# A build-time order made anew: another length for an exponential, another table of turns, three shifts at the end

## The chip, the cores and the metric

The kernel runs on one core of one Trainium2 chip. The metric is the device time of one execution in microseconds (us), as the median of several runs. The engines are called TensorE (PE in the profile, with its weight loads as PEld), VectorE (DVE), ScalarE (ACT), GpSimd (POOL) and SyncE (SP).

## The reference

The output mixes an attention block and a gated feed-forward block by a gate for each row. S = 2048 rows, D = 512 columns, 32 heads of 16, F = 1792. All inputs are bf16.

```python
x = A_x
g = sigmoid((x * gate_w).sum(-1, keepdims=True))
qkv = (x @ wqkv).reshape(B, S, 3, H, Dh).transpose(2, 0, 3, 1, 4)
q, k, v = qkv[0], qkv[1], qkv[2]
p = softmax(einsum("bhqd,bhkd->bhqk", q, k) * Dh ** -0.5)
a = einsum("bhqk,bhkd->bhqd", p, v).transpose(0, 2, 1, 3).reshape(B, S, D) @ wo
b = (silu(x @ w_gate) * (x @ w_up)) @ w_down
return g * a + (1 - g) * b
```

## The kernel before

**The work.** The attention is cut into units: 4 blocks of 512 queries by 8 groups of four heads, 32 units in all. Each unit runs over 16 key tiles of 128 keys, so there are 512 key tiles. For each, the scores (keys on the partitions, 4 x 512 columns) go through an exponential, and the result is multiplied with the values. The values carry a column of ones, so that the denominators come with the sums. Projections (kp, qp, vp), the feed-forward block (gu, dps) and the output projection (ops) are side work of TensorE, cut into pieces.

**Two ways to an exponential.** A key tile of ScalarE takes two score pairs: two score matmuls side by side fill the 1024 columns of an s_t tile (there are two such tiles in PSUM), and one ACTIVATE turns it into an e_t tile. Then a round of four value matmuls adds it to o_ps. A key tile of VectorE takes four d_t tiles of 512 columns. VectorE evicts each with a multiply and an add to 16-bit integers, whose bits are an approximate exponential in bf16. That result then becomes either four copies (three passes that add one of SHIFTS, and four rounds of value matmuls) or two copies (two passes that mask bits and one product, and two rounds). GpSimd takes strips of some passes and of the products. A d_t tile may ride in the same TensorE round as an s_t pair. The copies lie in c_t, kaug or wd_t, whichever buffer is free.

**The order.** Each engine's instructions are put in one fixed order when the program is built. A planner (the object plan) keeps a clock for each engine and books a cost on it with every instruction that it places: 0.217 us for a round on TensorE and FLIP = 0.107 for a change between score rounds and column rounds, 0.6 for an eviction on VectorE, and ACT_US for the exponential of an s_t tile on ScalarE. These clocks decide what is placed next. The pair emitter waits for the time at which the planner believes the s_t bank free (s_end), and before that fills TensorE's room with value rounds, side pieces and d_t tiles. The function v_unit decides whether another key tile goes to VectorE: it does so if VectorE's clock with its work in hand and a lead lies before the end of ScalarE's remaining tiles of the unit, reckoned from plan.act with TILE_US = 1.9 a tile. The chip sees none of these costs. It sees the order and the split between the engines.

```python
        def exp():
            act(out=e_t[:], in_=s_t[:], func=ACT.Exp, scale=inv_sqrt_dh)
            plan.act = max(plan.act, ready) + ACT_US
            s_end[i] = plan.act + SLOT
...
                end = plan.act + (left - 1) * TILE_US + ((hi[au] - at_) * TILE_US if vu > au else 0.0)
                busy = sum(v.cost for v in vops) + 0.6 * (len(owed) + len(d_wait))
                if plan.dve + busy + (LEAD if vu < UNITS - 1 else LAST) + {"h": -2.0, "i": 2.0}.get(turn_of(pairs[0]), 0.0) <= end:
                    return vu
```

**The table of turns.** TURNS holds two characters for each score pair, in the order in which the pairs are placed: one read by turn_of, one by way_of. A dot leaves the planner's rule as it is. A letter bends one rule at that pair. Of turn_of: a, b, c change how far TensorE may overrun the free bank; d lets no d_t tile ride along; e lets one take a bank that would be kept for side work; f and g change the credit for side work; h and i shift the lead in v_unit; j, k and o change which value round goes first; s holds back side pieces. Of way_of: f and g bear on two copies or four; l, m, o, d, r and u change what VectorE does first; n, q and t what GpSimd takes; v and w how much work VectorE may have in hand; x and y how early and how many d_t tiles may be placed.

**The end.** The last unit's last two key tiles are cut by halves of the queries. What follows them is placed by a small list of steps, each with an engine, a cost and the steps that it comes after with a gap: rc1 and rc0 are reciprocals of denominators, sp1 and sp0 their spread over the partitions by TensorE, n their product with the sums, p the last products with the output weights, c the copies out. LAST_HALF names the steps of the second half of the queries, which are preferred. Rounds of a rest of the output projection (al_o) are put between the steps where they fit.

Of the kernel before, what the change touches and what calls it, by code (L numbers as in the profile page):

```python
# [54 lines left out]
class Pacer:  # L55
# [30 lines left out]


TURNS = (
    ".......u................g.a.k...............i...a................n.....x...v..s................."
    "j............x.x....e....g.......r.r.g....c.c...a......x..................e....r.w.....y........"  # L90
    "......hn.x..............j.h.........if.....v.......m........k.............i....q..........a....."
    "....h.o..........r.........f..f.h.........gt.....uhm............................................"
    "....................j................................qb..g.r.............x.................y...."
    "........k.d............g.f......f..o...............w................hf................k..t...r.."
    "..........s.........h........w...f........................s............................g........"
    ".......g.......v...y...r........k......o........c..............................................."
    ".....d..........i.a......lo..g......e..t..e..v.......r.........................................."
    "............a..m....f...i.k......rk........x.......lk.............k..........d...............g.."
    "..............b....y........o......w.....u..e..f.....g....a....f.r..d.b.bl..............i.k....d"
    "...u....iq........k....ge................f..c....m..s...gu...mh..xbvj..x.wo...c.b..w.qbq.x..bw.."  # L100
    "bm.q..e.......cy...........r..o.....o.....h...........a..................u...w.w.......r..g....."
    "........b........gk..t...........f.xsykl...n..j.o...b...o....l.la......n......h...h..ddr..k.s.c."
    "a..g...rj.h...h....ds.....j...h......v...y.....l.....l....c..l...yb.i...ov.nb...i...a..l......k."
    ".u....k...elj.g...i.k.....j.o....lb.....fg.........qa.....c.a.fy..ku.r"
)


# [1 line left out]
def kernel(  # L109
# [86 lines left out]
    def act(*args, **kw):  # L196
        ordered(nc.scalar.activation(*args, **kw))  # L197
# [127 lines left out]
    plan = Plan()  # L325
# [5 lines left out]
    def spend(mode, mms, ready=0.0):  # L331

        plan.seq += 1
        work_at.append((plan.pe, mms))
        plan.pe = max(plan.pe + (FLIP if mode != plan.mode else 0.0), ready) + (0.226 if mode == "F" else 0.217) * mms
        plan.mode = mode
# [437 lines left out]
    def emit_pair(bs, ride=0):  # L774
# [17 lines left out]
# [4 lines that stand above are left out]
# [8 lines left out]
    KF = 2  # L804
# [6 lines left out]
    def emit_fin():  # L811
# [14 lines left out]
# [4 lines that stand above are left out]
# [36 lines left out]
        return TURNS[2 * n + 1] if 2 * n + 1 < len(TURNS) else "."  # L866

    exps = []
    ACT_US = 0.9167

    def flush_act(before=None):

# [408 lines left out]
    def spread_rows(p, rt, tqs=range(TQ), c0=0):  # L1281
        for tq in tqs:
            for j in range(4):
                mm(p[32 * j:32 * j + 32, c0 + tq * P:c0 + (tq + 1) * P],
                   lhsT=rt[:, 4 * tq + j:4 * tq + j + 1].broadcast_to([P, 32]), rhs=ident[:, :],
                   start=True, stop=True, tile_position=(0, 32 * j), skip_group_check=True)
# [4 lines left out]
    def last_rows(t):  # L1291
        cs = slice(t * P, (t + 1) * P)
        return lambda i: ((onc[QB - 1][:, i, cs], wo_t[:, i, :]) if i < NB - 1 else
                          (osbs[UNITS - 2][:, cs], wo_l[:, 0, :]) if i == NB - 1 else (ident[:, :], bblk[:, t, :]))
# [7 lines left out]
    rest = [(3, i) for i in range(NB + 1)]  # L1302

    def apart(p, w, r, start, stop):
        for j in range(4):
            mm(p[32 * j:32 * j + 32, 0:D], lhsT=w[:, 32 * j:32 * j + 32], rhs=r, start=start, stop=stop,
               tile_position=(0, 32 * j), skip_group_check=True)
# [504 lines left out]
    while au < UNITS:  # L1812
# [10 lines left out]
        if room > 0.02:  # L1823
# [29 lines left out]
            if room > 0.4 and not fin and closed in o_of and 0 < pvs[closed] and pv_left(closed) > 1 and (closed or pvs[0] != FT) and sum(  # L1853
                    w for t, w in work_at[-24:] if t > plan.pe - 3.0) < 6.5:

                for j in range(4):
                    mm(o_of[closed][32 * j:32 * j + 16, :], lhsT=vaug[:, 0, G * 4 * VC:], rhs=xT[:, 0, 0:QBW],
                       start=False, stop=False, tile_position=(0, 32 * j), skip_group_check=True)
# [58 lines left out]
    def fin_inv(h):  # L1917
        rt = work.tile([P, 4 * TQ], BF16, tag="rt", name="rt")
        recip16(rt[:, 8 * h:8 * h + 8], fin_l["p", h][:, 8 * h:8 * h + 8])
        fin_l["r", h] = rt  # L1920

    def fin_spread(h):
        spread_rows(fin_l["p", h], fin_l["r", h], (2 * h, 2 * h + 1), P - 2 * P * h)

    def fin_norm(tq, n=1):
        cs, c0 = slice(tq * P, (tq + n) * P), P + tq % 2 * P
        vec.tensor_tensor(out=on_l[:, cs], in0=osb[:, cs], in1=fin_l["p", tq // 2][:, c0:c0 + n * P], op=ALU.mult)
# [24 lines left out]
    LAST_HALF = ("os1", "dt1", "rc1", "sp1", ("n", 2), ("n", 3), ("p", 2), ("p", 3), ("v", 2 * KF - 1))  # L1952

    def step(name, engine, cost, f, *after):
        steps[name] = (engine, cost, f, after)
# [3 lines left out]
    step("os1", "A", 0.47, lambda: fin_copy(1), (("v", 2 * KF - 1), 0.25))  # L1959
    step("dt1", "F", 0.5, lambda: fin_dens(1), ("os1", 0.06))  # L1960
    step("rc1", "V", 0.22, lambda: fin_inv(1), ("dt1", 0.25))
    step("sp1", "C", 1.5, lambda: fin_spread(1), ("rc1", 0.3))
    for tq in (2, 3):
        step(("n", tq), "V", 0.23, lambda tq=tq: fin_norm(tq), ("sp1", 0.22))
        step(("p", tq), "C", 1.0, lambda tq=tq: fin_product(tq), (("n", tq), 0.06), (("l", tq), 0.0))
    step("dt0", "F", 0.5, lambda: fin_dens(0), ("os0", 0.06), ("s", 0.0))
    step("rc0", "V", 0.22, lambda: fin_inv(0), ("dt0", 0.25))
    step("sp0", "C", 1.5, lambda: fin_spread(0), ("rc0", 0.3))
    step("n0", "V", 0.37, lambda: fin_norm(0, 2), ("sp0", 0.22))
    for tq in (0, 1):  # L1970
        step(("p", tq), "C", 1.0, lambda tq=tq: fin_product(tq), ("n0", 0.06))
# [7 lines left out]
    al_at = lambda tq: s_end[1 - older] if "dt0" in over else 1e9  # L1979
    over["l", 2] = 0.0  # L1980
    now = {"V": plan.dve, "A": plan.act}
    while steps:
        able = {}
        for name, (engine, cost, f, after) in steps.items():
            if all(a in over for a, t in after):
                able[name] = max([now.get(engine, plan.pe)] + [over[a] + t for a, t in after])
        best = None
        for name, start in able.items():
            engine, cost = steps[name][:2]
            cost *= 0.217 if engine in "CF" else 1.0  # L1990
            if name not in LAST_HALF and any(able[o] + 0.06 < start + cost for o in able if o in LAST_HALF and (
                    steps[o][0] == engine or steps[o][0] + engine in ("CF", "FC"))):
                continue
            if best is None or start < best[0] - 0.02:
                best = start, name
        lim = min([max(plan.pe, max(over[a] + t for a, t in st[3])) for st in steps.values() if st[0] in "CF" and all(a in over for a, t in st[3])], default=1e9)
        if rest and not (best and best[0] <= plan.pe) and (best is None or best[1] != ("v", 2 * KF - 1)) and max(plan.pe, al_at(rest[0][0])) + 0.12 <= min(lim, 1e8):
            tq, i = rest.pop(0)
            if i == 0:
                a_ps.append(ps_s.tile([P, 2 * QBW], F32, tag="s", name="al_o"))  # L2000
            w, r = last_rows(tq)(i)
            apart(a_ps[tq], w, r, i == 0, False)
            spend("C", 1, al_at(tq))
            if not rest or rest[0][0] != tq:
                over["l", tq] = plan.pe
            continue
        start, name = best
        engine, cost, f, after = steps.pop(name)
        if engine in "CF":
            if name[0] == "v":  # L2010
                plan.pe = max(plan.pe, start)
                f()
                over[name[1]] = plan.pe
            else:
                f()
                spend(engine, cost, start)
            over[name] = plan.pe
        else:
            plan.dve = start
            f()  # L2020
            now[engine] = over[name] = start + cost
            plan.dve = now["V"]
# [34 lines left out]
```

## Time and profile before

| | |
|---|---|
| median of 3 runs | 742.37 us (741.66 to 742.51) |
| the profiled execution's own time | 742.09 us |
| its span, first to last instruction | 740.4 us |
| busy share of PE, DVE, ACT, POOL | 97%, 97%, 98%, 40% |
| exponentials on ScalarE (e_t from s_t) | 754, mean length 1098 ns |
| granted TensorE clock | 0.999 |

A row of the groups in the profile gives the source line, the engine, the operation, output and input by the program's names, their shapes and the count. Behind the first bar stand the busy time in us and the mean length of one in ns, behind the second the idle time of the engine just before these instructions, and what ended it. Nearly all instructions go through one helper for each engine, so the line numbers are those of the helpers (L194 TensorE, L197 ScalarE, L206 the others); groups are told apart by tile. An instruction's recorded length overlaps with the next one on the same engine, so lengths don't add up to time.

### The profile page before, as it was taken

The numbers are of one execution on the slowest core, as the hardware profiler recorded it, in microseconds if no ns is written. First come the engines' busy times: TensorE is split into PE (matmuls) and PEld (weight loads), VectorE is DVE, ScalarE is ACT, GpSimd is POOL, SyncE is SP. The second block draws the span as 40 slices with busy tenths as digits, with TensorE's granted clock in tenths as the row PEclk, the third lists the DMA queues.
The fourth block names the chain that finished last, engine by engine and source line by source line (L and its number), as shares of the span: only waits on it lengthen the run. The fifth ranks groups of instructions, "written<-read, shape, count | busy, mean of one in ns | idle before, by whom it ended". The sixth has DMA issues, their size and how long they took to land.

```text
span 740.4 us, 23142 instructions
## 1 busy us (share of the span) xinstructions
PE 721.8 (97%) x9296; PEld 213.6 (29%) x9296; DVE 715.5 (97%) x1223; ACT 728.4 (98%) x828; POOL 299.6 (40%) x370
## 2 busy tenths in 40 slices
PE   8999999999999999999999999999999999999997
PEld 3323222232222222322222222222222222222223
DVE  5999999999999999999999999999999999999995
ACT  7999999999999999999999999999999999999996
POOL 4044242234453336345444225544445255343441
PEclk9999999999999999999999999999999999999999
DMA  9001233355210012320200041302001231200001
GB/s 223 14 2 29 56 62 62 63 141 101 68 44 13 17 42 68 72 48 11 58 17 24 15 107 33 80 21 60 18 12 29 64 80 44 46 19 14 20 26 36
DMA packets 93523, 36.29 MB, mean 49 GB/s; under 512 B 76448, under 2 KB 92968, under 8 KB 93416
## 3 DMA queue, kind: packets, MB, share of 16 engines
q1 hardware_dynamic: 91688, 34.49, 20.0%
q8 instruction: 72, 1.18, 0.7%
q10 hardware_dynamic: 1728, 0.33, 0.2%
q14 instruction: 35, 0.29, 0.1%
HBM read 21.42 MB, written 2.35 MB: 32 GB/s over the span
## 4 chain that ended last, share of the span: by engine, by line
PE 59%; ACT 27%; issue 6%; DVE 6%; DMA 2%; ACTq 0%; DVEq 0%
ACT e_t L197 24%; PE s_t L194 21%; PE o_ps L194 17%; PE gu L194 7%; PE ops L194 6%; DVE c_t L206 3%; ACT th L197 2%; PE qp L194 2%; PE vp L194 2%; PE dps L194 1%; PE kp L194 1%; DVE mt L206 1%; DMA wqk<-in_A_wqkv_dram 1%; DVE kaug L206 1%; DMA rb<-in_A_wqkv_dram 1%
## 5 line engine op out<-in xcount | busy, mean ns | idle before, releaser
L197 ACT ACTIVATE e_t<-s_t 128x1024 bf16<-128x1024 f32 x754 | 704.1, 1098 | 0.6 <-PE s_t L194 0.2
L206 DVE TENSOR_SCALAR c_t<-d_t 128x512 uint16<-128x512 f32 x468 | 307.2, 681 | 3.4 <-PE d_t L194 2.7
L194 PE MATMUL s_t<-qx,kaug 32*128 32x512 bf16 (+2 forms) x1208 | 233.4, 383 | 9.6 <-ACT e_t L197 8.4
L206 POOL TENSOR_SCALAR c_t<-c_t 128x352 uint16<-128x352 uint16 (+19 forms) x210 | 149.0, 710 | 210.1 <-DVE c_t L206 141.5
L194 PEld LDWEIGHTS <-kaug 32*128 32x128 bf16 (+1 forms) x2056 | 80.6, 91 | 311.5 <-issue 308.3
L194 PE MATMUL d_t<-qx,kaug 32*128 32x512 bf16 x440 | 150.2, 384 | 0.0
L194 PE MATMUL o_ps<-e_t,vaug 128*32 128x512 bf16 (+2 forms) x1608 | 148.5, 372 | 0.0
L194 PE MATMUL o_ps<-c_t,vaug 128*32 128x512 bf16 (+2 forms) x1388 | 123.8, 372 | 0.2
L206 DVE TENSOR_SCALAR c_t<-c_t 128x2048 uint16<-128x2048 uint16 (+8 forms) x185 | 116.5, 641 | 0.5
L206 POOL TENSOR_TENSOR c_t<-c_t 128x480 bf16<-128x480 bf16 (+8 forms) x53 | 65.2, 1241 | 101.7 <-DVE c_t L206 69.9
L194 PEld LDWEIGHTS <-vaug 128*32 128x32 bf16 x3236 | 67.1, 95 | 104.7 <-issue 92.4
L194 PE MATMUL gu<-xT,wg 128*32 128x512 bf16 x896 | 72.1, 384 | 0.0
L194 PE MATMUL gu<-xT,wu 128*32 128x512 bf16 x896 | 66.5, 382 | 0.3 <-DVE kaug L206 0.2
L194 PE MATMUL ops<-wd_t,mt 128*32 128x512 bf16 x672 | 55.9, 382 | 0.0
L206 DVE TENSOR_TENSOR c_t<-c_t 128x1568 bf16<-128x1568 bf16 (+8 forms) x50 | 46.8, 937 | 0.0
L206 DVE SCALAR_TENSOR_TENSOR gs<-th,gu 128x512 bf16<-128x512 bf16 x56 | 38.0, 678 | 2.0 <-ACT th L197 1.9
L206 DVE TENSOR_SCALAR kaug<-d_t 128x512 uint16<-128x512 f32 x60 | 39.6, 682 | 0.0
L206 DVE SCALAR_TENSOR_TENSOR mt<-gs,gu 128x512 bf16<-128x512 bf16 x56 | 37.9, 677 | 0.5 <-PE gu L194 0.5
L197 ACT ACTIVATE th<-gu 128x512 bf16<-128x512 f32 x56 | 37.9, 677 | 0.0
L194 PE MATMUL s_t<-q,kaug 32*128 32x512 bf16 (+1 forms) x184 | 35.8, 385 | 1.0 <-ACT e_t L197 0.9
L194 PEld LDWEIGHTS <-mt 128*32 128x32 bf16 (+1 forms) x1058 | 24.6, 95 | 27.2 <-issue 21.4
L206 POOL TENSOR_SCALAR c_t<-kaug 128x1088 uint16<-128x1088 uint16 (+15 forms) x21 | 18.4, 875 | 26.0 <-DVE c_t L206 12.7
(151 smaller groups left out, 561.0 us busy)
## 6 DMA issues: line engine op xcount, KB each, us to landing
wg<-in_B_w_gate_dram SPq DMA_DIRECT2D x56, 128.0 KB
wu<-in_B_w_up_dram SPq DMA_DIRECT2D x56, 128.0 KB
on<-osb SPq DMA_DIRECT2D x120, 16.0 KB
rb<-rr SPq DMA_DIRECT2D x15, 128.0 KB
kaug<-kbt SPq DMA_DIRECT2D x28, 64.0 KB
wd_t<-in_B_w_down_dram SPq DMA_DIRECT2D x7, 256.0 KB
qx<-qst SPq DMA_DIRECT2D x96, 16.0 KB
qx<-aq SPq DMA_DIRECT2D x96, 16.0 KB
```

The costliest lines, as they stand in the source:

```text
L194: return ordered(nc.tensor.matmul(*args, **kw))
L197: ordered(nc.scalar.activation(*args, **kw))
L206: return lambda *a, **kw: ordered(f(*a, **kw))
```

## The change

The constant ACT_US, the cost that the planner books for an exponential, goes from 0.9167 to 0.906. The table TURNS is replaced: before it holds 247 letters, after it 144, and at one position alone the letter is the same. Among the steps of the end, the gap between a reciprocal and its spread goes from 0.3 to 0.35, a step outside LAST_HALF gives way to one of LAST_HALF that is able 0.2 us (before: 0.06) or more ahead of its end, and a round of the rest needs 0.17 us of room (before: 0.12).

```diff
 TURNS = (
-    ".......u................g.a.k...............i...a................n.....x...v..s................."
-    "j............x.x....e....g.......r.r.g....c.c...a......x..................e....r.w.....y........"
...
-    "a..g...rj.h...h....ds.....j...h......v...y.....l.....l....c..l...yb.i...ov.nb...i...a..l......k."
-    ".u....k...elj.g...i.k.....j.o....lb.....fg.........qa.....c.a.fy..ku.r"
+    ".....m.............x...nc..y........d..q...nk.....c.f..l.l.....g............b..................."
+    "..g......................d.........x.....d............d.f.ogc..................o............b..."
...
+    "..k....................................................f........................................"
+    "......d.....d.....................h"
 )
...
-    ACT_US = 0.9167
+    ACT_US = 0.906
...
-    step("sp1", "C", 1.5, lambda: fin_spread(1), ("rc1", 0.3))
+    step("sp1", "C", 1.5, lambda: fin_spread(1), ("rc1", 0.35))
...
-    step("sp0", "C", 1.5, lambda: fin_spread(0), ("rc0", 0.3))
+    step("sp0", "C", 1.5, lambda: fin_spread(0), ("rc0", 0.35))
...
-            if name not in LAST_HALF and any(able[o] + 0.06 < start + cost for o in able if o in LAST_HALF and (
+            if name not in LAST_HALF and any(able[o] + 0.2 < start + cost for o in able if o in LAST_HALF and (
                     steps[o][0] == engine or steps[o][0] + engine in ("CF", "FC"))):
...
-        if rest and not (best and best[0] <= plan.pe) and (best is None or best[1] != ("v", 2 * KF - 1)) and max(plan.pe, al_at(rest[0][0])) + 0.12 <= min(lim, 1e8):
+        if rest and not (best and best[0] <= plan.pe) and (best is None or best[1] != ("v", 2 * KF - 1)) and max(plan.pe, al_at(rest[0][0])) + 0.17 <= min(lim, 1e8):
```

More of the change, by code (lines that the diff above doesn't have):

```diff
@@ L88 @@
 TURNS = (
-    ".......u................g.a.k...............i...a................n.....x...v..s................."
-    "j............x.x....e....g.......r.r.g....c.c...a......x..................e....r.w.....y........"
-    "......hn.x..............j.h.........if.....v.......m........k.............i....q..........a....."
-    "....h.o..........r.........f..f.h.........gt.....uhm............................................"
-    "....................j................................qb..g.r.............x.................y...."
@@ L94 @@
[L94 to L102, printed above, removed]
-    "a..g...rj.h...h....ds.....j...h......v...y.....l.....l....c..l...yb.i...ov.nb...i...a..l......k."
@@ L104 @@
-    ".u....k...elj.g...i.k.....j.o....lb.....fg.........qa.....c.a.fy..ku.r"
+    ".....m.............x...nc..y........d..q...nk.....c.f..l.l.....g............b..................."
+    "..g......................d.........x.....d............d.f.ogc..................o............b..."
+    "....e.......................j.........a............................o...mi.......k..............."
+    ".......q...q......iy.x........g.......i.........s............................................x.."
+    ".....m.d...r.g.....o..............a.........o..f............................g..................."
@@ new lines @@
+    ".................d........g.............................b...............g.......k..............r"
+    "b....lar......................b...........f..........l...n...o.....g.......r......g...j...f....."
+    "..........f..........n.....................t...f......j..........t...............n....k........."
+    ".oc........m................j.......s..........u.........r....f...g..x........i...k.....hg......"
+    "...............f...q.............................o...y.........f......ao.q....sd.q......g......."
@@ new lines @@
+    "i...i...s............l....................................j....................................."
+    "...........................r.n...y................h...h................xb...b............oko...."
+    "s.....k...................d...........h..............f..j..w...........l.................t...o.."
+    "...y........o.................g..................w......j.d...........s........l................"
+    "..k....................................................f........................................"
```

## The prediction

> **What bounds the kernel now.** I read the page first, for the share of each engine.
>
> ```profile
> span 740.4 us, 23142 instructions
> PE 721.8 (97%) x9296; PEld 213.6 (29%) x9296; DVE 715.5 (97%) x1223; ACT 728.4 (98%) x828; POOL 299.6 (40%) x370
> ```
>
> Three engines are at 97 or 98%, so the table of stages comes next: head, two halves of the body, tail. Its columns are the stretch, its length, then busy us and instructions of PE, PEld, DVE, ACT and POOL.
>
> ```profile
> 0.00:10.70 10.70, 8.83 (x72) 4.78 (x72) 5.30 (x32) 5.35 (x12) 7.92 (x22) 1.00 0.92 175
> 10.70:380.00 369.30, 362.64 (x4672) 107.04 (x4671) 359.46 (x615) 369.06 (x417) 143.97 (x176) 1.00 0.24 55
> 380.00:731.80 351.80, 346.55 (x4483) 100.10 (x4487) 348.50 (x572) 351.62 (x396) 147.74 (x172) 1.00 0.15 39
> 731.80:740.40 8.60, 3.83 (x80) 1.64 (x68) 2.24 (x7) 2.33 (x5) 0.00 (x0) 0.93 0.19 61
> ```
>
> In the 721.1 us of the body ScalarE is idle for 0.4 us by this count, VectorE for 13.1, TensorE for 11.9. ScalarE looks like the bound. But its count hides waits, as the groups, the view of its line and its timeline show (start, length, engine, line, operation, count):
>
> ```profile
> L197 ACT ACTIVATE e_t<-s_t 128x1024 bf16<-128x1024 f32 x754 | 704.1, 1098 | 0.6 <-PE s_t L194 0.2
> L197 ACT ACTIVATE e_t<-s_t x754: 1018/1094/1294, 10.7 to 730.7; 128x1024 bf16<-128x1024 f32 x189
> 10.74 17.63 ACT L197 ACTIVATE e_t<-s_t 128x1024 bf16<-128x1024 f32 x19 [0.18 <-PE s_t L194]
> 213.02 47.88 ACT L197 ACTIVATE e_t<-s_t 128x1024 bf16<-128x1024 f32 x52
> 299.50 0.59 ACT L197 ACTIVATE th<-gu 128x512 bf16<-128x512 f32 x1
> 299.98 3.80 ACT L197 ACTIVATE e_t<-s_t 128x1024 bf16<-128x1024 f32 x4
> 445.22 4.70 ACT L197 ACTIVATE e_t<-s_t 128x1024 bf16<-128x1024 f32 x5
> 504.67 6.53 ACT L197 ACTIVATE e_t<-s_t 128x1024 bf16<-128x1024 f32 x7
> ```
>
> One exponential lasts 1.098 us, yet in a run of several one starts much sooner after the other: take the last one's length off a run and divide by the steps. That gives (4.70 - 1.098)/4 = 0.9005 us in the run of 5, 0.905 in the run of 7, but (47.88 - 1.098)/51 = 0.9173 in the run of 52. A delay of up to about 0.18 us hides in the overlap. The first starts at 10.74, the last at 730.7: 720.0 us. A tanh takes 299.98 - 299.50 = 0.48 of that, and there are 56: 26.9. So 753 steps took 693.1 us, **0.9204 each**. The order written at build time allows 0.9167. Against the quickest runs (0.903, the mean of the two) ScalarE lost 753 x 0.0174 = 13 us, as much as the others lost. All three are in lockstep with some 12 us of slack each; none alone is the limit.
>
> ```profile
> PE s_t L194 <- ACT e_t L197: 9.7, 30, 0.9
> ACT e_t L197 <- PE s_t L194: 0.2, 1, 0.2
> DVE c_t L206 <- PE d_t L194: 2.7, 9, 0.8
> ```
>
> The waits (total, times, longest) say the same: TensorE waits for ScalarE's banks 30 times, 9.7 us in all, and elsewhere it is TensorE that comes late by less than the overlap hides.
>
> From this comes the formula used below. With N exponentials at a mean step c, the time is 742.37 + (N - 1) x c - 693.1. The profiled execution took 742.09: 10.74 before the first exponential, 720.0 to the last one's start, 9.7 from there to the end of the span, 1.7 outside it. It stands 0.28 under the median of 742.37; differences are worked out on it and set against the median.
>
> **The change: the constant.** It alters no instruction's form or length on the chip, only what the order believes, and through that N, the mix of work and c. Believing 0.906 instead of 0.9167, the order's ScalarE line is 754 x 0.0107 = 8.07 us shorter. What the others must do to follow needs the price of a key tile (two exponentials on ScalarE, or one tile by bit tricks on VectorE).
>
> ```profile
> L206 DVE TENSOR_SCALAR c_t<-d_t 128x512 uint16<-128x512 f32 x468 | 307.2, 681 | 3.4 <-PE d_t L194 2.7
> L206 DVE TENSOR_SCALAR kaug<-d_t 128x512 uint16<-128x512 f32 x60 | 39.6, 682 | 0.0
> L206 DVE TENSOR_SCALAR wd_t<-d_t 128x512 uint16<-128x512 f32 x12 | 8.1, 681 | 0.1
> L206 DVE TENSOR_SCALAR c_t<-c_t 128x2048 uint16<-128x2048 uint16 (+8 forms) x185 | 116.5, 641 | 0.5
> L206 DVE TENSOR_TENSOR c_t<-c_t 128x1568 bf16<-128x1568 bf16 (+8 forms) x50 | 46.8, 937 | 0.0
> L206 DVE TENSOR_SCALAR kaug<-c_t 128x2048 uint16<-128x2048 uint16 (+3 forms) x42 | 27.8, 663 | 0.0
> L206 DVE TENSOR_SCALAR c_t<-kaug 128x2048 uint16<-128x2048 uint16 (+2 forms) x29 | 18.8, 658 | 0.1
> L206 DVE TENSOR_TENSOR kaug<-c_t,kaug 128x1568 bf16<-128x1568 bf16 (+4 forms) x14 | 13.7, 980 | 0.0
> L206 DVE TENSOR_TENSOR c_t<-kaug,c_t 128x2048 bf16<-128x2048 bf16 (+3 forms) x9 | 8.9, 984 | 0.0
> ```
>
> Four d_t evictions make a tile, so 540 of them are 135 tiles: 354.9 us, 2.63 a tile. The six larger groups of passes add 232.5 us, 1.72 a tile. A tile costs VectorE 4.35 us, ScalarE two steps, 1.81 by the new order.
>
> ```profile
> L194 PE MATMUL o_ps<-c_t,vaug 128*32 128x512 bf16 (+2 forms) x1388 | 123.8, 372 | 0.2
> L194 PE MATMUL o_ps<-kaug,vaug 128*32 128x512 bf16 (+2 forms) x216 | 20.9, 376 | 0.0
> L194 PE MATMUL o_ps<-wd_t,vaug 128*32 128x512 bf16 x20 | 2.0, 383 | 0.0
> 401.08 0.39 PE L194 MATMUL s_t<-qx,kaug 64*128 64x512 bf16 x2
> 401.40 0.40 PE L194 MATMUL ops<-wd_t,mt 128*32 128x512 bf16 x4
> 401.63 0.39 PE L194 MATMUL o_ps<-kaug,vaug 128*32 128x512 bf16 x4
> 401.95 0.39 PE L194 MATMUL s_t<-qx,kaug 64*128 64x512 bf16 x2
> ```
>
> Values for VectorE's tiles: 1624 matmuls, four to a round, so 406 rounds, 3.0 a tile (those with four copies take 4, with two copies 2). A round is about 0.22 us on TensorE, a score round between two column rounds 0.87 - 2 x 0.22 = 0.43. A tile that goes to ScalarE costs TensorE two score rounds more and two value rounds less: 0.86 - 0.43 = +0.43. A tile turned from four copies to two saves TensorE 0.43 and costs VectorE 0.3 to 0.5 (two passes of 0.63 and a product of 0.94 to 1.2, for three passes of 0.63); I take 0.4.
>
> If x tiles go to ScalarE and y tiles turn to two copies, all three lines shorten by the same t when t = 8.07 - 1.81x, t = 4.35x - 0.4y and t = 0.43y - 0.43x. That gives **x = 2.1, y = 12, t = 4.3 us**, N = 758: the shortest order that this constant allows if VectorE, TensorE and GpSimd are used as fully as now. Of the 8.07 us, 3.8 go back into the two tiles.
>
> Does the chip follow? Now each exponential has 0.012 to 0.016 in hand (0.9167 against the quickest runs), and after a late score tile ScalarE catches up out of that; at 0.906 only 0.001 to 0.006 is left. The unknown is c: not under 0.903, not over the 0.9204 of now. I take the middle between the order's 0.906 and the longest run's 0.9173: 0.9117. Then 757 x 0.9117 = 690.2, 2.9 less than 693.1: **739.5 us**. The Trainium skill (Perfetto Trace Analysis, Optimizing Scalar/DVE Operations) gives ScalarE about 51 ns on PSUM beside its elements; with the 0.83 ns an element of ScalarE: Activation LUTs, Rules for kernel authors, I estimate 0.90 us. The two quickest runs agree; the run of 52 does not.
>
> **The table.** 247 letters become 144, and only one position keeps its letter. A letter shifts a single decision: how much TensorE may overrun, whether a d_t tile rides along, two copies or four, what VectorE does first. Letters that force two copies fall from 9 to 6, those that give that choice to the free buffers from 13 to 5. None adds an instruction of its own, but every decision behind a changed one may fall otherwise, so N and c are drawn anew. No row prices this. Its bounds: one tile better (N = 756) or two worse (N = 762) than the balance, 1.8 or 3.7 us of ScalarE; I take the balance and keep both for the range. The DMAs that SyncE issues stay the same in number, and no wait on one lies in the body's waits above; if one came late, its consumer on TensorE would wait, and up to 0.18 us of that would be hidden.
>
> **The tail.** The three shifts bear only on the 8.6 us after the body.
>
> ```profile
> 733.78 0.21 DVE L206 RECIPROCAL rt<-dt 128x8 bf16<-128x8 f32 x1 [0.91 <-PE dt L194]
> 734.12 0.39 PE L194 MATMUL al_o<-bblk,ident 128*32 128x512 bf16 x4
> 734.33 0.28 PE L194 MATMUL dt<-ident,rt 128*32 128x128 bf16 x8
> 734.74 0.48 DVE L206 TENSOR_TENSOR on_l<-osb,dt 128x128 bf16<-128x128 bf16 x2 [0.46 <-PE dt L194]
> ```
>
> From the reciprocal's end at 733.99 to the spread are 0.34 us; the steps now say 0.35 rather than 0.3, with a projection round between them. Such a round is 0.21 us. At best one leaves the chain, at worst two enter: -0.2 to +0.4. I take nothing, since the round stands in the wait already.
>
> **The rivals.** *The order's reserve is handed back.* N rises to 758, and c comes down only to 0.9157, as late score tiles, earlier hidden by the reserve, now hold ScalarE: 757 x 0.9157 = 693.2, 742.5 us. For it: ScalarE took more than the 0.9167 allowed even with 0.012 in hand. Against: TensorE stood waiting for ScalarE 9.7 us.
>
> *More on ScalarE than the time gained: slower.* The order gives VectorE tiles by whether it would be done before ScalarE; a ScalarE believed faster keeps more. If the new table does not win them back, x = 4, N = 762, at the 0.9185 that the first run of 19 shows ((17.63 - 1.098)/18): 761 x 0.9185 = 699.0, 748.3 us. It decides where (N - 1) x c passes 693.1: at 0.9117 from N = 762 on, at 0.9173 from 757. For it: VectorE, TensorE and ScalarE are so evenly loaded that an order not as finely fitted loses at once, and the new table steers in fewer places. Against: VectorE has 13.1 us idle to win tiles with. The Trainium skill speaks for this rival: Perfetto Trace Analysis, Identifying the Most-Contended Engine, says to relieve the engine with the highest occupancy, here ScalarE with 98%, and this change loads it.
>
> *ScalarE runs at its floor.* With c = 0.905, the run of 7, 757 x 0.905 = 685.1 and 734.4 us. Against: TensorE and VectorE would have to give 8 us of their 12 or 13 idle. The skill's estimate of 0.90 above would come out here.
>
> **How the numbers follow.** About 0.2%, 1.5 us, is what a measurement can tell from no change. Forecast, 736.5 to 740.9: 0.39. Floor, under 736.5: 0.07. Handed back, 740.9 to 743.9: 0.15. Slower, over 743.9: 0.39. So faster 0.46, same 0.15, slower 0.39. The forecast is the likeliest by a hair; both signs hold much. Its own range is 736.5 to 740.9. The 8-in-10 range leaves out half of the floor case and the worst sixth of all: 735 to 748.
>
> **What would show it.** Right: 756 to 760 exponentials, 135 tiles down to 132 to 134 (528 to 536 d_t evictions), fewer than 406 value rounds for them, a step near 0.912, and waits of TensorE for ScalarE not above 9.7 us. The tail stays at 8.6 us within 0.4. Wrong on N: 762 or more. Wrong on c: a step of 0.916 or over, with TensorE and VectorE idle in the body for as long as now or longer. A tail that moves by over a microsecond would say the three shifts were not small.

## The result and the profile after

The changed kernel is slower: a median of 750.92 us (747.37 to 751.25) against 742.19 us, a ratio of 1.0107 (95% interval 1.0076 to 1.0139). The forecast was 739.5 us, the range 735 to 748. The profiled execution took 751.12 us, 9.03 more than that of before.

The page of the changed kernel, its groups of the exponentials and of VectorE's evictions, and the view of ScalarE's line (lengths in ns: shortest, median, longest):

```profile
span 749.4 us, 22885 instructions
PE 726.5 (97%) x9192; PEld 216.6 (29%) x9192; DVE 713.9 (95%) x1213; ACT 733.7 (98%) x834; POOL 272.5 (36%) x336
L197 ACT ACTIVATE e_t<-s_t 128x1024 bf16<-128x1024 f32 x760 | 711.5, 1137 | 6.0 <-PE d_t L194 4.9
L206 DVE TENSOR_SCALAR c_t<-d_t 128x512 uint16<-128x512 f32 x464 | 306.0, 683 | 9.3 <-PE d_t L194 7.8
L206 DVE TENSOR_SCALAR kaug<-d_t 128x512 uint16<-128x512 f32 x48 | 31.4, 683 | 0.1
L206 DVE TENSOR_SCALAR wd_t<-d_t 128x512 uint16<-128x512 f32 x16 | 10.9, 684 | 1.3 <-PE d_t L194 1.3
L197 ACT ACTIVATE e_t<-s_t x760: 1018/1132/1317, 10.9 to 741.4; 128x1024 bf16<-128x1024 f32 x190
```

There are 760 exponentials instead of 754, and 528 evictions instead of 540: three key tiles went from VectorE to ScalarE. All three busy engines have their work of before within 1%, and the span is 9 us longer.

**What an exponential costs.** The prediction took ScalarE's pace from the starts in a run. The ends say something else. A tanh ends 444.74 + 0.59 = 445.33, and the five exponentials after it, quoted in the prediction as a quick run, end at 445.22 + 4.70 = 449.92: 0.918 us each. The run of seven ends at 511.20, after a tanh that ended at 504.79: 0.916 each. These are the two tanh rows, from ScalarE's timeline in the kernel before:

```profile
444.74 0.59 ACT L197 ACTIVATE th<-gu 128x512 bf16<-128x512 f32 x1
504.20 0.59 ACT L197 ACTIVATE th<-gu 128x512 bf16<-128x512 f32 x1
```

The same timeline in the changed kernel has a long run after its last tanh:

```profile
672.14 0.69 ACT L197 ACTIVATE th<-gu 128x512 bf16<-128x512 f32 x1
672.61 68.97 ACT L197 ACTIVATE e_t<-s_t 128x1024 bf16<-128x1024 f32 x75
```

Here 75 exponentials end at 741.58, the tanh before them at 672.83: 68.75 / 75 = **0.9167 each**, over 69 us. The starts come sooner, about 0.903 after each other, while the recorded lengths grow within a run, from 1.018 up to 1.294 us before and 1.317 after. The starts run ahead of the ends and fall back again; only the ends keep one pace. In both kernels the median distance between the ends of two neighbouring exponentials is 0.917 us and the shortest 0.913. So 0.9167 is what an exponential of this size occupies ScalarE for in this kernel, the old constant was exact, and 0.906 is a pace that no pair of ends shows.

**Where the time went.** Counted at ends, ScalarE needs (N - 1) x 0.9167 + 56 x 0.49 (a tanh, by its ends). Before, the first exponential ends at 11.77 and the last at 731.82: 720.05 us, of which 717.7 are needed and 2.3 lost. After, it is 11.89 to 742.50: 730.61, with 723.2 needed and 7.4 lost. The stages before, cut at these ends (columns as in the prediction):

```profile
11.77:731.82 720.05, 708.81 (x9150) 207.03 (x9153) 706.91 (x1183) 719.68 (x811) 291.71 (x348) 1.00 0.20 47
731.82:740.40 8.58, 3.81 (x80) 1.64 (x68) 2.22 (x7) 2.31 (x4) 0.00 (x0) 0.93 0.19 61
```

And after:

```profile
11.89:742.50 730.61, 713.91 (x9060) 209.95 (x9060) 705.65 (x1174) 724.81 (x817) 264.60 (x314) 1.00 0.20 46
742.50:749.40 6.90, 2.96 (x58) 1.35 (x57) 1.86 (x5) 2.42 (x4) 0.00 (x0) 1.00 0.24 78
```

Six exponentials more: +5.5. Lost by ScalarE: +5.1. The tail: 8.58 to 6.90, -1.7. The head: +0.1. Together 9.0.

**The 5 us lost** lie nearly all in one place. From the timeline of the changed kernel, three issues of SyncE, and then what stood idle (in brackets, with what ended it):

```profile
146.46 6.11 SPq L206 DMA_DIRECT2D qx<-qst  x8
152.67 5.09 SPq L206 DMA_DIRECT2D qx<-aq  x8
157.86 1.69 SPq L206 DMA_DIRECT2D wg<-in_B_w_gate_dram  x1
161.66 1.04 PE L194 MATMUL gu<-xT,wg 128*32 128x512 bf16 x8 [3.40 <-DMA wg<-in_B_w_gate_dram]
163.35 1.02 ACT L197 ACTIVATE e_t<-s_t 128x1024 bf16<-128x1024 f32 x1 [3.82 <-PE d_t L194]
163.74 1.29 DVE L206 TENSOR_SCALAR c_t<-d_t 128x512 uint16<-128x512 f32 x2 [4.39 <-PE d_t L194]
```

The stages there, and then a finer cut around the stop; the last three columns are the granted clock, the DMA share and GB/s:

```profile
150.00:158.00 8.00, 7.88 (x103) 2.41 (x102) 7.97 (x13) 8.00 (x10) 3.56 (x5) 1.00 0.12 30
158.00:161.60 3.60, 0.26 (x2) 0.00 (x0) 1.35 (x3) 1.53 (x2) 0.00 (x0) 0.77 0.37 80
161.60:167.40 5.80, 5.74 (x48) 1.14 (x48) 3.09 (x5) 3.56 (x4) 0.48 (x1) 0.56 0.93 251
158.26:159.91 1.65, 0.00 (x0) 0.00 (x0) 1.09 (x2) 1.27 (x2) 0.00 (x0) 1.00 0.05 11
159.91:161.66 1.75, 0.00 (x0) 0.00 (x0) 0.00 (x0) 0.00 (x0) 0.00 (x0) 0.50 0.73 154
161.66:166.74 5.08, 5.08 (x40) 1.00 (x44) 3.00 (x5) 2.90 (x4) 0.00 (x0) 0.50 0.91 250
```

Sixteen issues of query rows hold SyncE's queue for over 11 us. In the kernel before, a pair of weights goes out between the two groups of eight:

```profile
141.56 5.35 SPq L206 DMA_DIRECT2D qx<-qst  x8
147.01 0.53 SPq L206 DMA_DIRECT2D wg<-in_B_w_gate_dram  x1
147.63 0.45 SPq L206 DMA_DIRECT2D wu<-in_B_w_up_dram  x1
148.18 4.94 SPq L206 DMA_DIRECT2D qx<-aq  x8
```

In the changed kernel the gate weight stands behind all sixteen and is issued at 157.86, and TensorE, whose next instruction needs it, stands for 3.40 us. Its granted clock falls to 0.50 at 159.91, 1.65 us into the stop, and stays there for 6.8 us, until 166.74. From 161.6 to 167.4 TensorE gets through 48 matmuls; with the weights earlier it gets through 74 (next section). The Trainium skill (TensorE: Matmul & The Clock Gate, Why this matters for your kernels) warns of idle gaps over about 3 us, with which the clock falls; the trace agrees for a gap of 3.40 us, though here the clock fell before the gap was 3 us old. Of the four runs three had a mean clock of 0.994 or 0.995 and took 750.73 to 751.25 us; the fourth had 1.0 and took 747.37.

### The profile page after: what moved, and what is told of

Its sections match the earlier page's. It is cut to its first block, busy times and chain, and to the rows that moved or that the text cites. A ratio compares the mean times of both kernels' runs of the same rounds, so it can differ in the third digit from the quotient of the medians.

```text
span 749.4 us, 22885 instructions
## 1 busy us (share of the span) xinstructions
PE 726.5 (97%) x9192; PEld 216.6 (29%) x9192; DVE 713.9 (95%) x1213; ACT 733.7 (98%) x834; POOL 272.5 (36%) x336
## 4 chain that ended last, share of the span: by engine, by line
PE 43%; ACT 43%; issue 9%; DVE 3%; DMA 1%; SPq 0%; ACTq 0%
ACT e_t L197 40%; PE s_t L194 15%; PE o_ps L194 12%; PE gu L194 8%; PE ops L194 3%; ACT th L197 3%; DVE c_t L206 1%; PE kp L194 1%; PE qp L194 1%; PE vp L194 1%; PE dps L194 1%; PE warm L194 1%; DMA wg<-in_B_w_gate_dram 1%; ACT mt L197 0%; DVE mt L206 0%
## 5 line engine op out<-in xcount | busy, mean ns | idle before, releaser
L197 ACT ACTIVATE e_t<-s_t 128x1024 bf16<-128x1024 f32 x760 | 711.5, 1137 | 6.0 <-PE d_t L194 4.9
L194 PE MATMUL s_t<-qx,kaug 32*128 32x512 bf16 (+2 forms) x1208 | 234.3, 383 | 10.5 <-ACT e_t L197 8.2
L206 POOL TENSOR_SCALAR c_t<-c_t 128x384 uint16<-128x384 uint16 (+18 forms) x157 | 114.7, 731 | 185.7 <-DVE c_t L206 138.5
L194 PEld LDWEIGHTS <-kaug 32*128 32x128 bf16 (+1 forms) x2056 | 86.1, 91 | 315.7 <-issue 311.4
L194 PE MATMUL o_ps<-e_t,vaug 128*32 128x512 bf16 (+3 forms) x1584 | 149.2, 377 | 0.6 <-DVE vaug L206 0.5
L206 POOL TENSOR_TENSOR c_t<-c_t 128x480 bf16<-128x480 bf16 (+9 forms) x61 | 69.1, 1145 | 161.9 <-DVE c_t L206 95.5
L206 DVE TENSOR_SCALAR c_t<-c_t 128x2048 uint16<-128x2048 uint16 (+5 forms) x190 | 121.3, 650 | 0.3
L194 PE MATMUL o_ps<-c_t,vaug 128*32 128x512 bf16 (+2 forms) x1304 | 118.2, 376 | 0.4 <-DVE vaug L206 0.4
L206 DVE TENSOR_TENSOR c_t<-c_t 128x1568 bf16<-128x1568 bf16 (+9 forms) x56 | 55.5, 991 | 0.0
L206 DVE TENSOR_SCALAR kaug<-d_t 128x512 uint16<-128x512 f32 x48 | 31.4, 683 | 0.1
L206 POOL TENSOR_SCALAR kaug<-c_t 128x352 uint16<-128x352 uint16 (+12 forms) x36 | 24.4, 678 | 18.4 <-DVE c_t L206 13.6
```

Source lines behind the costliest of these rows:

```text
L194: return ordered(nc.tensor.matmul(*args, **kw))
L206: return lambda *a, **kw: ordered(f(*a, **kw))
```

## The experiments

My theory was that the time is the number of exponentials times a step that the constant doesn't change, plus the late weight; its rivals were the tail and the new table by itself. What sets the step was a question of its own. At first I still held, with the prediction, that ScalarE could go at 0.903 and that late score tiles kept it from that; the rival was ScalarE's own pace. The section above has the answer; the fourth, fifth and sixth kernel below bear on it.

**The three shifts alone.** Constant and table are those of before.

```diff
-    step("sp1", "C", 1.5, lambda: fin_spread(1), ("rc1", 0.3))
+    step("sp1", "C", 1.5, lambda: fin_spread(1), ("rc1", 0.35))
...
-            if name not in LAST_HALF and any(able[o] + 0.06 < start + cost for o in able if o in LAST_HALF and (
+            if name not in LAST_HALF and any(able[o] + 0.2 < start + cost for o in able if o in LAST_HALF and (
...
-        if rest and not (best and best[0] <= plan.pe) and (best is None or best[1] != ("v", 2 * KF - 1)) and max(plan.pe, al_at(rest[0][0])) + 0.12 <= min(lim, 1e8):
+        if rest and not (best and best[0] <= plan.pe) and (best is None or best[1] != ("v", 2 * KF - 1)) and max(plan.pe, al_at(rest[0][0])) + 0.17 <= min(lim, 1e8):
```

> The kernel before with only the three shifts among the last operations; constant and table are the old ones. Theory (the count of exponentials and a late weight load make the change slow, the tail is small): 741.7 to 742.6, within 0.5 us of before, and the same 754 exponentials. Rival (the tail order costs part of the 8.7 us): 744 or more, with the 8.6 us after the body grown by 2 or more.

Measured: 741.66 against 742.09 us, ratio 0.9995 (0.9985 to 1.0004), 754 exponentials. The stage after the last exponential's end, 8.58 before, is

```profile
731.63:739.50 7.87, 3.94 (x80) 1.64 (x68) 2.27 (x7) 2.42 (x4) 0.00 (x0) 1.00 0.20 67
```

0.7 us shorter in the profiled execution; the medians can't tell it from no change. The shifts are not the cause of the longer time.

**The weights one chain earlier**, in the changed kernel. The order of the compute engines stays the same.

```diff
-    ffnw = ctx.enter_context(tc.tile_pool(name="ffnw", bufs=4))
+    ffnw = ctx.enter_context(tc.tile_pool(name="ffnw", bufs=5))
...
-        for i in range(3):
+        for i in range(4):
             w_load(i, True)
...
-                w_load(i + 3, True)
-                w_load(i + 3, False)
+                w_load(i + 4, True)
+                w_load(i + 4, False)
```

> The changed kernel with the gate and up weights loaded four chains ahead instead of three (five buffers instead of four); the order of the four compute engines stays the same, only SyncE issues two loads earlier and keeps two ahead. Theory: the stop of TensorE at 158 to 161.7 us and the lower clock after it go; 751 falls by about 5 to 745 to 747, granted clock 1.0, still slower than before by 3 to 5 us since 760 exponentials at a step of 0.917 to 0.920 remain. Rival (the stop is no cause of its own, the new order is late everywhere): under 2 us gained, 749 or more.

Measured: 745.53 us (745.42 to 746.1), ratio 1.0049 (1.0034 to 1.0064), clock 1.0. The stages at the same place:

```profile
158.00:161.60 3.60, 3.60 (x48) 0.96 (x45) 3.33 (x6) 3.60 (x6) 0.00 (x0) 1.00 0.50 121
161.60:167.40 5.80, 5.79 (x74) 1.61 (x74) 5.80 (x10) 5.80 (x7) 2.78 (x2) 1.00 0.95 241
```

TensorE does not stop here and the clock stays full. The stop, with the lower clock, was worth 5.4 us. How the 5.4 divide between the two is not shown. What is left, 3.4 us, is the six exponentials (5.5) less the shorter tail (1.7) and 0.4 of small terms: ScalarE's ends, at which this stage is cut, span 725.2 us, with 2.0 lost, as little as before:

```profile
11.60:736.81 725.21, 711.90 (x9060) 209.88 (x9060) 705.47 (x1174) 724.30 (x817) 264.59 (x314) 1.00 0.20 46
```

**The new table with the old constant.**

```diff
-    ACT_US = 0.906
+    ACT_US = 0.9167
```

> The changed kernel with the constant back at 0.9167, new table and tail kept. The table then meets other states and the order places 770 exponentials instead of 760. Theory (the chip takes a step of about 0.918 whatever the constant): (769 x 0.918 - 693.1) + 742.4 = 755 us, up to 760 with a late load; step between 0.916 and 0.921. Rival (the new table itself makes ScalarE late, at any constant): a step of 0.925 or more outside single stops, 761 or more. Second rival (the constant sets the step): 0.928, 763.

Measured: 757.85 us (755.81 to 758.43), ratio 1.0209 (1.0194 to 1.0224), with 770 exponentials.

```profile
L197 ACT ACTIVATE e_t<-s_t 128x1024 bf16<-128x1024 f32 x770 | 719.5, 1114 | 0.5 <-PE s_t L194 0.4
11.46:745.58 734.12, 719.67 (x9154) 213.55 (x9157) 694.73 (x1156) 733.83 (x828) 203.48 (x254) 1.00 0.20 46
```

In the profiled execution (755.81 us) the ends run from 11.46 to 745.58, 734.1 us, of which 769 x 0.9167 + 27.4 = 732.4 are needed: 1.7 lost. In this execution neither the new table nor the constant makes ScalarE late. They decide how many exponentials it gets, and sixteen more than before are 14.7 us, against 13.7 between the two profiled executions. The other three runs took 2.0 to 2.6 us more than the profiled one; why is not shown. The counts hold a surprise: the new table raises N from 754 to 770 at the old constant, and the lower constant then brings it down to 760. That is the other way from the prediction, in which a ScalarE believed faster gets more. The old table with the new constant was not run, so no more can be said of each one's part.

**Thin value rounds.** The kernel before, with TensorE relieved: most value matmuls cover 64 columns only, so the kernel leaves out most of the value sums.

```diff
-            mm(o[32 * j:32 * j + 32, cols], lhsT=vaug[:, n % KT, v0:v0 + 32], rhs=e[:, cols],
+            cc = cols if first or last else slice(c0, c0 + 64)
+            mm(o[32 * j:32 * j + 32, cc], lhsT=vaug[:, n % KT, v0:v0 + 32], rhs=e[:, cc],
```

> The kernel before with all value matmuls but the first and last of a unit narrowed to 64 columns, so that most of the value sums are left out; ScalarE, VectorE and GpSimd keep their instructions and order. TensorE gets some 70 to 100 us of room. Theory (ScalarE can step at 0.903 to 0.92 and is held by late score tiles): the mean step falls from 0.920 to 0.905 to 0.913, 731 to 738 us. Rival (ScalarE itself needs 0.917 or more beside the others): step 0.917 to 0.920, 740 to 742.

Measured: 749.44 us, ratio 1.01 (1.0077 to 1.0124), which neither expected. The page's TensorE clock, a wait in the whole span and the same wait between 674 and 735 us, and a run of ScalarE:

```profile
PEclk9999999999999999997999999999999999999999
PE s_t L194 <- ACT e_t L197: 82.4, 293, 1.0
PE s_t L194 <- ACT e_t L197: 7.5, 27, 0.5
673.39 0.63 ACT L197 ACTIVATE th<-gu 128x512 bf16<-128x512 f32 x1
673.87 61.58 ACT L197 ACTIVATE e_t<-s_t 128x1024 bf16<-128x1024 f32 x67
```

TensorE, less busy, was granted a mean clock of 0.972, so the total is no answer. Inside it lies one: TensorE waited 293 times for ScalarE, 82.4 us, 27 times of them and 7.5 us in the stretch shown, and still the 67 exponentials after the tanh that ended at 674.02 ended at 735.45, 0.917 each. With TensorE waiting for it, ScalarE was no faster. This speaks against a floor at 0.903, my theory, and for the rival. Whether ScalarE would go faster if the other engines did nothing at all was not tried.

**Shorter exponentials**, before and (with the weights one chain earlier) after. If ScalarE needs 0.9167 for 1024 columns, it is to need less for 1012, and the new constant becomes true.

```diff
-            act(out=e_t[:], in_=s_t[:], func=ACT.Exp, scale=inv_sqrt_dh)
+            act(out=e_t[:, 0:1012], in_=s_t[:, 0:1012], func=ACT.Exp, scale=inv_sqrt_dh)
...
+            cc = slice(c0, min(c1, 1012 - QBW)) if k is None and i % 2 else cols
...
```

Both kernels leave out the scores of the last 12 queries of each block in every second head (columns are queries; the first expectation below calls them keys). A few matmuls are added to start the sums of those columns: 10 in the old order, 4 in the new.

> The kernel before with each exponential but the last four cut from 1024 to 1012 columns; the last 12 keys' columns of every second head are left out of the sums. Same order, same 754 instructions. Theory (an exponential occupies ScalarE for 0.9167 us, read from end to end, and ScalarE is the bound at that rate): end to end goes to 0.9167 x (1012 + 76)/(1024 + 76) = 0.9067, up to 754 x 0.010 = 7.5 us less where TensorE and VectorE follow in an order made for 0.9167: 735 to 739. Rival (ScalarE's own time is 0.903 already, and late score tiles set the step): under 1.5 us less, 740.5 to 742.5.

> The changed kernel with the weights one chain earlier and the exponentials cut to 1012 columns in the same way, so that one takes about what the new constant says (0.9067 against 0.906). Theory: the order now believes the truth, and the lag behind it that grew by 0.010 us an exponential goes: 745.5 - 760 x 0.010 = 738, 736.5 to 739.5, the end-to-end step 0.907. Rival (the new order is late for reasons of its own): 742 or more.

Measured: 739.83 us for the old order, ratio 0.9969 (0.9958 to 0.9981); 738.97 us for the new one, ratio 0.9958 (0.9944 to 0.9973). Runs of ScalarE in the old and in the new order:

```profile
662.69 0.63 ACT L197 ACTIVATE th<-gu 128x512 bf16<-128x512 f32 x1
663.17 67.09 ACT L197 ACTIVATE e_t<-s_t 128x1012 bf16<-128x1012 f32 x73
```

```profile
660.70 0.61 ACT L197 ACTIVATE th<-gu 128x512 bf16<-128x512 f32 x1
661.18 69.16 ACT L197 ACTIVATE e_t<-s_t 128x1012 bf16<-128x1012 f32 x76
```

In the new order 76 of them, the last four at full width, take 730.34 - 661.31 = 69.0 us, 0.908 each. Over the whole trace the median distance between two ends is 0.907, in either order: twelve columns less make 0.010 us less. The changed kernel with the weights earlier falls from 745.53 by 6.6 us: it was ScalarE's pace that held it. In the old order 73 take 730.26 - 663.32 = 66.9, 0.917 each: some exponentials there come late, so the order itself holds ScalarE back, and only 2.3 of 7.5 us are gained. That is 0.8 over the range that I had given. Behind ScalarE, then, the other engines were close in the old order. The two bodies come out equal. The old order, cut from the first end to the last:

```profile
11.70:730.26 718.56, 708.88 (x9160) 205.57 (x9163) 705.77 (x1183) 716.52 (x811) 291.72 (x348) 1.00 0.20 47
```

and the new one:

```profile
11.53:730.33 718.80, 707.82 (x9064) 205.98 (x9064) 701.84 (x1174) 717.43 (x817) 264.63 (x314) 1.00 0.20 47
```

With 718.6 and 718.8 us, even with the ScalarE it believes in, the new order gains only in the tail (8.45 to 6.90 us). The old order's profiled execution had a clock of 0.50 for 3.4 us and took 740.72 us, 0.9 over its median, so its body is, if anything, a little shorter.

## Why the prediction was wrong

**ScalarE's pace is the step that failed.** "The quickest runs (0.903)" subtracted one mean length from a run and divided by the steps. That measures the distance between starts, and it took for free time what is the growth of the recorded lengths. "ScalarE lost 13 us" should have been 2.3. With it fell "none alone is the limit": ScalarE was the limit, all but saturated, and the idle time of TensorE and VectorE was no sign that it could go faster. (Close behind it they were, as the shorter exponentials show.) The middle value 0.9117 for c was under a floor. In the formula, counted by starts, c came out at 0.9204 before, at 0.927 in the changed kernel with its stop, and at 0.920 with the weights earlier, unchanged. The term that I had priced at -2.9 us was +10.5 in the changed kernel, and +5.1 without the stop.

The figures of the Trainium skill (Perfetto Trace Analysis, Optimizing Scalar/DVE Operations; ScalarE: Activation LUTs, Rules for kernel authors), set beside it, gave an estimate of 0.90 us; by its ends the trace gives 0.9167, so that the fixed part is nearer to 0.067 than to 0.051 us if a column costs 0.83 ns, with which the shorter exponentials agree (0.010 us for 12). The measurement decides. The Trainium skill's other rule, to optimize the engine with the highest occupancy first (Perfetto Trace Analysis, Identifying the Most-Contended Engine), was borne out in the changed kernel: the order loaded ScalarE, and each exponential cost its full length.

**The order's counts came out, but not by the working.** N = 760 lies in "756 to 760", three tiles moved where 2.1 were worked out, and the value rounds of VectorE's tiles fell from 406 to 387 ((1304 + 228 + 16) / 4):

```profile
L194 PE MATMUL o_ps<-c_t,vaug 128*32 128x512 bf16 (+2 forms) x1304 | 118.2, 376 | 0.4 <-DVE vaug L206 0.4
L194 PE MATMUL o_ps<-kaug,vaug 128*32 128x512 bf16 (+2 forms) x228 | 21.8, 373 | 0.0
L194 PE MATMUL o_ps<-wd_t,vaug 128*32 128x512 bf16 x16 | 1.6, 382 | 0.0
```

By the third experiment the fit of N looks like luck: at the new table the lower constant took ten exponentials from ScalarE, where the working has it add four. At 3.0 rounds a tile three tiles are 9 of the 19 rounds, so the other 10 are about five tiles turned to two copies, where y = 12 was worked out. And the gain t = 4.3 us is not to be seen in the order: with the weights earlier, VectorE is busy 705.5 us between ScalarE's first and last end (706.9 before) and TensorE 711.9 (708.8 before), where both were to shorten by 4.3. With the shorter exponentials the new order's body is no shorter than the old one's either.

**The DMAs.** "No wait on one lies in the body's waits" was read from the kernel before and carried over to an order in which every issue stands elsewhere. The count stayed, the place didn't, and a stop of 3.4 us with the lower clock after it cost 5.4. The 0.18 us of cover was right in kind (ends keep their pace over a start that comes a little late) and about twenty times too small for a wait of 3.4 us.

**The tail** came out at -1.7 us where -0.2 to +0.4 was given. In the profiled execution the three shifts alone give 0.7 of it, which the medians don't tell from nothing. The rest hangs on the order that leads there: with the same shifts and the new table, but the old constant, the tail is 8.4 us. Which part of the order does it was not tried.

**The rival "more on ScalarE"** named the sign, the price and the turning point: at 0.9173, slower from N = 757 on. Its reason for a larger N, a ScalarE believed faster, isn't borne out by the third experiment. The rival had no late weight in it; without that, N = 760 gives 745.5, and the weight makes up the rest to 750.9.

## What to carry to other kernels

Take an engine's pace from ends, over a run that begins behind another instruction's end, and check whether the recorded lengths stay the same within the run: where they grow, starts run ahead and the difference is no slack. A constant in a build-time order that is below what the engine needs does not make the engine faster. What it does to the split between the engines has to be counted, together with the table that it works with: here the new table gave ScalarE more work, and at that table the lower constant gave it less. And an order made anew moves the DMA issues too: look for a weight behind a long row of small issues, and for what the clock does after the stop.

## What the runs showed of the hardware

An exponential of 128 x 1024 from PSUM to bf16 occupies ScalarE for 0.9167 us and one of 1012 columns for 0.907, end to end in this kernel, while starts follow at 0.903 and 0.893 and the recorded length grows by 0.013 us from one to the next, up to about 1.3 us, before it falls back. In a stop of TensorE of 3.40 us its granted clock fell to 0.50 after 1.65 us and stayed there for 6.8 us, 5.1 of them behind the stop.
